# Memory rows and ride rows issued from ScalarE's queue, row pairs for the 64-row parts of T, and another order

## The chip, the cores and the metric

The kernel runs on one core of one Trainium2 chip. Its engines are TensorE (PE, with its weight loads as PEld), VectorE (DVE), ScalarE (ACT), GpSimd (POOL) and SyncE (SP), each with a queue of its own that is worked off in order. The metric is device time in microseconds (us) of one execution, as a median of several. A profiled execution gives the trace from which the durations below are read.

## The reference

Two layer pairs, each of them a recurrent attention A and a gated MLP B, on 2048 tokens of width 448:

```python
x = x + A(layernorm(x));  x = x + B(layernorm(x))
x = x + A(layernorm(x));  x = x + B(layernorm(x))

# A: 64 segments of 32 tokens, 16 heads of 256, memory of 8 rows
mem = mem0
for s in range(64):
    h = concat([mem, xs])                      # 40 rows
    q, k, v = h Wq, h Wk, h Wv                 # per head
    p = softmax(mask(q k^T / 16))
    o = sum over heads of (p v) Wo
    mem, out_s = o[:8], o[8:]
# B
h = relu(x W_gate) * (x W_up);  out = h W_down
```

The 8 memory rows of a segment are needed by the next one, so the segments of a layer form a chain. The two A layers use the same weights.

## The kernel before, in words

**Folded weights.** In the setup the kernel makes M = Wq Wk^T / 16 and N = Wv Wo for each head, so that a segment needs T = M h, the scores T^T h, U = p h and the output U N. M's 448 rows are cut into three parts of 128 and one of 64. The 64-row parts lie in the tensor M3, two blocks in one slot: one in partitions 0 to 63, one in 64 to 127 (PLACE, beside BLOCKS, L1042).

**Steps.** The program has 68 steps t (step, L1382). Step t works on segment t of layer 0 and on segment t - 4 of layer 1 side by side (LAG = 4), so most matmuls of T have 2 x 40 = 80 columns; in the first four and last four steps only one layer is at work, with 40. One step holds, by function:
- m_nat (L1201): six small DMAs that carry the memory rows mv, made by the step before. Four (L1211) put 8 rows by half the width each into hK, which the products U read; two (L1218) put 16 rows by half the width each into ride, from where L1221 (DVE) adds them to x of layer 1's rows in XB.
- t_block (L980), three times: T for blocks of units. Its inner function first() makes the 64-row parts of a block as matmuls that run beside each other in parts of the array, the rest the three 128-row parts. Each unit's PSUM bank is copied out by t_copies (L1024) into TTm and TTs, by ScalarE or DVE.
- s_mem (L1054), p_t_mem, u_mem, un_mem (L1158), m_t (L1178): the memory rows' attention and their output. un_mem is 112 matmuls; its halves are added by ScalarE (sumA) and DVE (mv, L1176). m_t transposes mv by matmuls, and DVE copies it into hT for the next step's T.
- s_seg (L1076), seg_pt, u_seg (L1231): the same for the segment's 32 rows. PTs is made by a DMA transpose. u_seg's four products per layer go to PSUM and are copied into big and UTm by ScalarE or DVE.
- In every second step un (L1274) makes U N for two segments, and then ln_b, b_layer, ln_a follow: layer norms, whose xBT and xAT come from DMA transposes (tdma, L975), and the MLP on a tile of 128 tokens.

**What sets the order.** No engine's order is written out. Each operation is recorded with the engines that may run it and a cost in ns (add); _Order.run (L391) is a list scheduler that takes the operations by due time (SLOT, keyed by function and step mod 4, period 86000 ns, with BIAS added) and by when its cost figures say that the engine, the PSUM bank and the inputs are free. For the steady steps (8 to 63) the TensorE order is pinned by SLOT. What comes out is one fixed instruction list for each engine, with semaphore waits (_Sched). Among the cost figures are 500 ns for a DMA issued from SP (qdma, L891), 1200 ns for a DMA transpose (tdma), and 120 ns for a DMA issued from ScalarE, which before the change only the six loads at the start use (small, L697). TensorE's cost figures have 95 ns for a change of tile shape ("mode": 0 full array, 1 for 64 rows by 128 columns, 2 for 32 columns, 3 for 64 by 64).

## Time and profile before

| | us |
|---|---|
| median of 3 runs | 1539.51 (1538.65 to 1540.07) |
| the profiled execution | 1535.5 |
| its span | 1533.6 |
| TensorE busy (matmul) | 1477.1 |
| VectorE busy | 803.6 |
| ScalarE busy | 777.2 |
| GpSimd busy | 112.8 |

The granted TensorE clock was 0.994 of full speed over the span. "Span" is the time from the first to the last instruction that the profile shows; the difference to the execution's own time lies around it. Issuing a DMA is not counted as busy time of an engine, but it occupies its queue: SP's queue held 461 copies and 146 transposes, ScalarE's six copies. Matmuls overlap, so the time of one kind is better read from the starts in the timeline than from its busy time. In the timelines a line has the start, the time until the last of the group ended, the engine (SPq and ACTq are queues that issue a DMA), the line of the code, the operation, output<-input, and the number of instructions.

### The profile page before, as it was taken

The numbers are of one execution on the slowest core, as the hardware profiler recorded it, in microseconds if no ns is written. First come the engines' busy times: TensorE is split into PE (matmuls) and PEld (weight loads), VectorE is DVE, ScalarE is ACT, GpSimd is POOL, SyncE is SP. The second block draws the span as 40 slices with busy tenths as digits, with TensorE's granted clock in tenths as the row PEclk, the third lists the DMA queues.
The fourth block names the chain that finished last, engine by engine and source line by source line (L and its number), as shares of the span: only waits on it lengthen the run. The fifth ranks groups of instructions, "written<-read, shape, count | busy, mean of one in ns | idle before, by whom it ended". The sixth has DMA issues, their size and how long they took to land.

```text
span 1533.6 us, 88464 instructions
## 1 busy us (share of the span) xinstructions
PE 1477.1 (96%) x41047; PEld 1157.1 (75%) x41051; DVE 803.6 (52%) x2198; ACT 777.2 (51%) x2491; POOL 112.8 (7%) x259
## 2 busy tenths in 40 slices
PE   6999889999999999999999999999999999999998
PEld 2577777878787887878687787878787788878675
DVE  6544545545554555645554554545455564555554
ACT  6644444555545554554555455554555455554433
POOL 4000000000000000000000000000000000000000
PEclk9999999999999999999999999999999999999999
DMA  9741001111110111111010110011010110011010
GB/s 219 185 126 29 17 16 22 22 16 19 22 22 16 24 17 21 22 17 19 16 24 17 24 21 16 19 22 22 17 24 17 22 22 17 18 20 21 17 21 14
DMA packets 137761, 48.24 MB, mean 31 GB/s; under 512 B 125736, under 2 KB 137264, under 8 KB 137392
## 3 DMA queue, kind: packets, MB, share of 16 engines
q1 hardware_dynamic: 137040, 42.33, 14.1%
q8 instruction: 323, 5.29, 1.4%
q14 instruction: 46, 0.38, 0.1%
q10 hardware_dynamic: 352, 0.24, 0.1%
HBM read 10.33 MB, written 1.84 MB: 8 GB/s over the span
## 4 chain that ended last, share of the span: by engine, by line
PE 83%; DVE 5%; DMA 4%; SPq 3%; ACT 3%; issue 1%
PE b L139 83%; SPq L690 3%; DMA PTs<-Ps 2%; DVE big L865 1%; DMA xBT<-xn 1%; ACT UTm L864 1%; ACT Em L1069 1%; DVE UTm L865 1%; DMA xAT<-xn 1%; SPq L1211 1%; DMA ride<-mv 0%; DVE mv L1176 0%; DVE Es L1111 0%; DMA Nw<-in_A_Wo_dram 0%; ACT sumA L864 0%
## 5 line engine op out<-in xcount | busy, mean ns | idle before, releaser
L139 PE MATMUL b<-hT,Mw 128*128 128x80 bf16 (+1 forms) x11424 | 438.6, 200 | 5.3 <-issue 4.1
L139 PEld LDWEIGHTS b<-hT,Mw 128*128 128x128 bf16 x11424 | 418.3, 100 | 19.2 <-issue 7.7
L139 PE MATMUL b<-Nw,big 128*32 128x448 bf16 (+1 forms) x3840 | 294.0, 353 | 1.9 <-DMA Nw<-in_A_Wo_dram 0.7
L864 ACT ACTIVATE TTm<-b 128x80 bf16<-128x80 f32 (+5 forms) x639 | 149.2, 234 | 273.8 <-PE b L139 266.1
L864 ACT ACTIVATE TTs<-b 128x320 bf16<-128x320 f32 (+5 forms) x640 | 269.0, 420 | 5.3 <-PE b L139 4.9
L139 PE MATMUL b<-xBT,big 128*128 128x128 bf16 (+3 forms) x4900 | 207.9, 215 | 4.1 <-DMA xBT<-xn 4.0
L139 PEld LDWEIGHTS b<-Nw,big 128*32 128x32 bf16 (+1 forms) x3840 | 131.3, 97 | 105.2 <-issue 10.3
L139 PE MATMUL b<-Nw,UTm 128*32 128x224 bf16 x7504 | 197.2, 263 | 6.4 <-ACT UTm L864 5.0
L139 PEld LDWEIGHTS b<-Nw,UTm 128*32 128x32 bf16 x7504 | 178.7, 98 | 29.3 <-ACT UTm L864 13.0
L139 PEld LDWEIGHTS b<-xBT,big 128*128 128x128 bf16 (+1 forms) x4900 | 182.6, 101 | 19.0 <-DMA xBT<-xn 4.7
L865 DVE CAST TTm<-b 64x64 bf16<-64x64 f32 (+4 forms) x245 | 54.6, 223 | 200.1 <-PE b L139 196.0
L139 PE MATMUL b<-hT,M 64*64 64x80 bf16 (+3 forms) x6808 | 145.9, 199 | 2.3 <-DVE hT L865 1.4
L864 ACT ACTIVATE big<-b 128x512 bf16<-128x512 f32 (+1 forms) x228 | 111.1, 544 | 60.8 <-PE b L139 60.4
L865 DVE CAST big<-b 128x512 bf16<-128x512 f32 (+1 forms) x160 | 97.3, 624 | 64.0 <-PE b L139 63.3
L139 PEld LDWEIGHTS b<-hT,M 64*64 64x64 bf16 (+2 forms) x6808 | 110.7, 107 | 26.6 <-issue 16.5
L864 ACT ACTIVATE UTm<-b 128x512 bf16<-128x512 f32 (+2 forms) x173 | 87.2, 541 | 64.8 <-PE b L139 64.0
L865 POOL COPY hK<-xn 32x448 bf16<-32x448 bf16 x136 | 75.3, 554 | 573.7 <-DVE xn L918 567.4
L865 DVE CAST TTs<-b 64x256 bf16<-64x256 f32 (+5 forms) x244 | 102.6, 420 | 5.4 <-PE b L139 5.4
L1343 DVE TENSOR_TENSOR hB<-gT,b 128x512 bf16<-128x512 bf16 (+2 forms) x128 | 78.0, 619 | 47.9 <-ACT gT L1342 26.8
L139 PE MATMUL b<-big,hB 128*128 128x448 bf16 (+1 forms) x574 | 100.0, 353 | 0.8 <-DVE hB L1343 0.8
L1342 ACT ACTIVATE gT<-b 128x512 bf16<-128x512 f32 (+2 forms) x128 | 66.4, 539 | 65.0 <-DVE hB L1343 34.1
L864 ACT ACTIVATE sumA<-b 64x224 f32<-64x224 f32 x67 | 23.7, 354 | 135.3 <-PE b L139 135.2
(101 smaller groups left out, 1328.6 us busy)
## 6 DMA issues: line engine op xcount, KB each, us to landing
hK<-mv SPq DMA_DIRECT2D x252, 3.5 KB
big<-in_A_Wo_dram SPq DMA_DIRECT2D x3, 896.0 KB, 5.9
ride<-mv SPq DMA_DIRECT2D x124, 7.0 KB, 1.8
out_dram<-ys SPq DMA_DIRECT2D x32, 56.0 KB, 2.0
big<-in_B_W_up_dram SPq DMA_DIRECT2D x7, 224.0 KB, 3.1
big<-in_B_W_gate_dram SPq DMA_DIRECT2D x7, 224.0 KB, 3.8
big<-in_B_W_down_dram SPq DMA_DIRECT2D x7, 224.0 KB, 3.4
XA<-in_A_x_dram SPq DMA_DIRECT2D x28, 56.0 KB, 2.2
```

The costliest lines, as they stand in the source:

```text
L139: ins = E.matmul(out, lhsT=lhsT, rhs=rhs, **kw)
L690: S.q.add("dma", ("sp",), {"sp": 6200.0 if w == "Wv" and q else 4100.0}, lambda E: E.dma_start_transpose(out=st[w, q], in_=src[w][:, q * 1 ...
L864: return E.activation(out(), src(), ACT.Copy, **({} if scale is None else {"scale": scale}))
L865: return E.tensor_copy(out(), src()) if scale is None else E.tensor_scalar(out(), src(), scale, None, op0=ALU.mult)
L1069: S.act(lambda E, i=i: E.activation(S.Em[:, i, :], src()[:, i, :], ACT.Exp, bias=st[:, 32 + i:33 + i], scale=1.0, accum_out=st[:, 34 + i:3 ...
L1211: S.qdma(f"mk{l}{n}", lambda E, a=a, b=b, n=n: E.dma_start(S.hK[a:a + 8, pp, s, DH * n:DH * n + DH], S.mv[b:b + 8, :]), [("hKm", pp, s, l, ...
L1342: S.act(lambda E, g=g, R=R, n=n: E.activation(S.gT[:, g, 0:n], R[0].b()[:, 0:n], ACT.Relu), n, R[0].res(), [("gT", g)])
L1343: S.dve(lambda E, g=g, R=R, n=n, fcs=fcs: E.tensor_tensor(S.hB[:, fcs[0]:fcs[-1] + 1, 0:w], S.gT[:, g, 0:n].rearrange("p (a b) -> p a b", ...
```

## The change

The six small DMAs of m_nat are recorded with adma and not qdma: ScalarE issues them, with a cost of 120 ns each in the scheduler. t_block's first() makes each 64-row part as one matmul of 64 rows by 128 columns of the array, two of which (partitions 0 to 63 and 64 to 127) stand in a pair, where two 64x64 matmuls each made it before. The tables BIAS and SLOT have new numbers; the period stays. The line numbers behind the tables grow by 2 to 5.

```diff
-    "t_blockm+": 4131, "t_blocks+": 6194, "s_mem+": -350, "p_t_mem+": 7632, ...
+    "t_blockm+": -901, "t_blocks+": -588, "s_mem+": -9244, "p_t_mem+": 9533, ...
...
+    def adma(self, name, fn, wr, rd=()):
+        self.q.add("dma", ("act",), {"act": 120.0}, fn, rd, wr, name=name, lat=2200.0)
...
                 for j in range(units[a][2]):
-                    for o, x in ((0, a), (0, b), (1, a), (1, b)) if l1 - l0 == 2 else ((-1, a), (-1, b)):
+                    for x in (a, b):
                         c, u0, m = units[x]
                         side, slot = S.PLACE[16 * c + u0 + j]
-                        h, g = slice(64 * side, 64 * side + 64), slice(64 * o, 64 * o + 64) if o >= 0 else slice(0, 128)
-                        out.append(MM(R[x].b()[g, j * n:j * n + n], S.M3[h, slot, g], mov(3, h), start=(j == 0), stop=False))
+                        h = slice(64 * side, 64 * side + 64)
+                        out.append(MM(R[x].b()[:, j * n:j * n + n], S.M3[h, slot, :], mov(3, h), start=(j == 0), stop=False))
...
-            S.mm(first, ..., mode=3 if l1 - l0 == 2 else 1)
+            S.mm(first, ..., mode=1)
...
-                S.qdma(f"mk{l}{n}", lambda E, a=a, b=b, n=n: E.dma_start(S.hK[a:a + 8, pp, s, DH * n:DH * n + DH], S.mv[b:b + 8, :]),
+                S.adma(f"mk{l}{n}", lambda E, a=a, b=b, n=n: E.dma_start(S.hK[a:a + 8, pp, s, DH * n:DH * n + DH], S.mv[b:b + 8, :]),
...
-                S.qdma(f"ride{n}", lambda E, a=a, b=b, n=n: E.dma_start(S.ride[a:a + 16, DH * n:DH * n + DH], S.mv[b:b + 16, :]), [("ride", w, n)], [("mem",)])
+                S.adma(f"ride{n}", lambda E, a=a, b=b, n=n: E.dma_start(S.ride[a:a + 16, DH * n:DH * n + DH], S.mv[b:b + 16, :]), [("ride", w, n)], [("mem",)])
```

## The prediction

> **What bounds the kernel now.** I read the page's busy shares first, then the chain of work that ended last, then the list of who waited for whom, and last the timelines of single steps.

> ```profile
> PE 1477.1 (96%) x41047; PEld 1157.1 (75%) x41051; DVE 803.6 (52%) x2198; ACT 777.2 (51%) x2491; POOL 112.8 (7%) x259
> ...
> PE b L139 83%; SPq L690 3%; DMA PTs<-Ps 2%; DVE big L865 1%; DMA xBT<-xn 1%; ACT UTm L864 1%; ACT Em L1069 1%; DVE UTm L865 1%; DMA xAT<-xn 1%; SPq L1211 1%; DMA ride<-mv 0%; DVE mv L1176 0%; DVE Es L1111 0%; DMA Nw<-in_A_Wo_dram 0%; ACT sumA L864 0%
> ```

> TensorE is busy 96% of the span and makes 83% of the chain, so the order keeps it fed. Adding up the gaps between matmul starts that exceed the usual gap of their kind gives some 39 us of stall in 1533.6 us, 1.2 us in a good period of four steps (86.6 us) and 2 to 3 us in a poor one (88.5 us). All that a better order can win lies in these 39 us; what makes TensorE wait longer is lost in full. Idle time of ScalarE (49%) is spread over the step, and whether it can take more work depends on when.

> **What the moved DMAs cost ScalarE.** The change moves 252 memory-row issues (hK<-mv) and 124 ride issues from SP to ScalarE, six per step. SP's own price for them, and what an issue from ScalarE takes (the only six in this trace, at the start), stand in the SP and ACT timelines; the source view of line 1211 has the spread:

> ```profile
> L1211 SPq DMA_DIRECT2D hK<-mv x252: 624/635/1480, 78.1 to 1503.2; - x126
> ```
> ```profile
> 1309.19 1.23 SPq L1218 DMA_DIRECT2D ride<-mv  x2
> 1310.46 3.25 SPq L1211 DMA_DIRECT2D hK<-mv  x4
> ```
> ```profile
> 0.75 1.28 ACT L629 ACT_TABLE_LOAD   x1 [0.75 <-PEq L1427]
> 0.78 0.56 ACTq L829 DMA_DIRECT2D XA<-in_A_x_dram  x1
> 1.37 0.77 ACTq L705 DMA_DIRECT2D ys<-in_A_mem_dram  x1
> 2.18 0.28 ACTq L706 DMA_DIRECT2D ys<-in_A_mem_dram  x1
> 2.50 1.77 ACTq L829 DMA_DIRECT2D XA<-in_A_x_dram  x3
> ```

> The reader is to see that issues stand one behind the other on ScalarE's queue as on SP's (0.78 + 0.56 ends at 1.34, the next begins at 1.37): 0.28 to 0.77 us each. What ran beside them was work already dispatched (the table load), nothing behind them. So the price per issue is bounded by 0.28 and 0.77 us; I take 0.66 us, the pitch of the same transfers on SP (0.635 us and 0.59 us busy, 0.67 and 0.62 us from one to the next), because rows, bytes and memories are the same. Six issues hold ScalarE's queue for 4 x 0.67 + 2 x 0.62 = 3.9 us. The planner that made the order counts 0.12 us each, 0.7 us for six: so the order leaves room for 0.7 us.

> [...]

> **What waits behind the six issues.** The order of the changed kernel is periodic: four kinds of step, the six issues in ScalarE's queue right after mv. A step of kind A (t mod 4 = 0) has the same TensorE order there as now, so the timelines of now (PE, ACT, DVE, SP) price it:

> ```profile
> 1284.47 0.84 PE L139 MATMUL b<-PTs,hK 40*64 40x512 bf16 x12
> ...
> 1286.83 0.53 PE L139 MATMUL b<-hT,M 64*64 64x80 bf16 x40
> 1287.29 1.36 PE L139 MATMUL b<-hT,Mw 128*128 128x80 bf16 x33
> ```
> ```profile
> 1284.59 0.35 ACT L864 ACTIVATE sumA<-b 64x224 f32<-64x224 f32 x1 [3.49 <-PE b L139]
> 1284.97 1.57 ACT L864 ACTIVATE UTm<-b 128x512 bf16<-128x512 f32 x3
> ```
> ```profile
> 1284.93 0.69 DVE L865 CAST big<-b 128x512 bf16<-128x512 f32 x1 [3.75 <-PE b L139]
> 1285.54 0.37 DVE L1176 TENSOR_TENSOR mv<-b,sumA 64x224 bf16<-64x224 f32 x1
> ```
> ```profile
> 1285.94 2.64 SPq L1211 DMA_DIRECT2D hK<-mv  x4
> ```

> Time from un_mem's end (1284.47): mv is done at +1.44, the first issue starts at +1.47, TensorE begins the next T block (hT,M) at +2.36, into banks that include the one of the third UTm eviction. Now that eviction ends at +2.07. In the changed order two UTm evictions stand ahead of the issues and the third behind them.

> - **A**: issues end at 1.47 + 3.9 = 5.4, the eviction (0.6 plus 0.1 of hand-over) at 6.1; TensorE could start at 2.36: stall 3.75 us.
> - **B** (t mod 4 = 1): issues right after sumA and mv, 0.9 to 4.85; then an eviction of big, done at 5.5. TensorE has ahead of the U product that reads it 8 x 0.38 (8 matmuls 128x448 each, 56 such in 2.66 us) + 0.45 (u_seg) = 3.5 us: stall 2.0 us.
> - **C** (mod 2): issues to 4.85, relu 0.4, four pairs TTm and TTs of 0.54 each, done at 7.5. TensorE ahead of the block that needs those banks: 30 gate/up matmuls x 0.056, m_t 0.2, ten row pairs 0.37, 84 matmuls x 0.0366, switches 0.3 = 5.6 us: stall 1.9 us.
> - **D** (mod 3): four issues, three evictions, two issues; the evictions end at 5.2, TensorE asks at 5.2: stall 0 to 0.1 us.

> That is 7.7 us per four steps, and 14 periods (t = 8 to 62) have it: 108 us. The first steps and the last carry the same issues in another order; I count nothing for them. After each burst ScalarE catches up within the T blocks (in A its queue is done with the first five banks at 9 us, when TensorE asks), so a stall isn't paid twice. By the bounds: at 0.28 us each A stalls 1.5 us and the others nothing, 21 us in all; at 0.77 us the four stall 4.45, 2.7, 2.6 and 0.4 us, 142 us in all.

> **What the moved DMAs free.** SP loses 376 issues, 246 us of issue time (252 x 0.66 and 124 x 0.64), so its transposes (xBT, xAT, PTs), x loads and y stores no longer stand behind them. What is that worth? In poor periods the chain runs from mv over four hK issues and a ride issue to the ride's landing (2.1 us) and the xBT transpose (4.2 us), where TensorE waits 1.1 us. On ScalarE the ride still stands behind the four memory rows, so this chain grows no shorter; but a TensorE held up by 3.75 us no longer waits at its end. I count 10 us of today's 39 us of stall as covered by the new ones or gone with SP's queue, between 0 and 20. The landing of the memory rows is no issue: the next u_mem reads them over 10 us later.

> **Row pairs.** In each step 100 matmuls 64x64 (25 sets of four) become 50 of 64 rows by 128 columns; 3000 matmuls and weight loads go. But a set of four takes 37.8 to 38.9 ns now (40 matmuls in 0.36 us), because four run beside each other. The trace has the new shape at 40 columns, in the first steps:

> ```profile
> 93.84 0.42 PE L139 MATMUL b<-hT,M 64*128 64x40 bf16 x20
> 94.19 1.40 PE L139 MATMUL b<-hT,Mw 128*128 128x40 bf16 x48
> ```

> Twenty in 0.35 us with the switch behind them: 25.4 ns a pair, what one full 128x128 matmul takes at 40 columns. So at 80 columns a pair should take the 36.6 ns of a full one: 25 x 1.7 ns x 60 steps = 2.5 us less. A change of tile shape costs 95 ns beyond the pitch between 64x64 and full, 83 to 87 ns for 64x128: 4 x 10 ns x 60 = 2.4 us less; the new order has 818 such changes instead of 803, 1.4 us more. Together -3 us; were the pairs to run singly it would be +55 us, which the row excludes.

> **The order.** Apart from the burst it differs little: as many evictions (ScalarE 22 more, DVE 22 fewer), 112 quarter matmuls for 28 full ones in un. Nothing for it, +-10 us.

> **Sum**, against the profiled execution (1535.5 us, of which 1533.6 span): 1535.5 + 108 - 10 - 3 = 1630.5; the median lies 4.0 above that execution: **1635 us**. In this case 1605 to 1668.

> **Rivals.**
> - *The issue is cheap on ScalarE (faster).* If an issue holds ScalarE's queue for under 0.13 us, as the planner counts, A stalls less than 6 x 0.13 - 0.18 = 0.6 us per period, below what SP's queue and the pairs give back; then 1539.5 - 3 - 10 = 1526 us. Place: the time from mv's end to the next ScalarE activation. For it: SP's queue is on the chain (1%) and goes. Against it: the six ACT rows, the shortest of them 0.28 us. Chance 0.12, nearly all below 1536.
> - *Short issues.* 0.28 to 0.5 us, like the shortest ACT row: 1539.5 + 21 - 13 = 1548 up to 1605. Chance 0.15, a fifth of it within 0.2%.
> - *Both queues hold each other up.* On SP a ride behind a transpose took up to 1.5 us instead of 0.59; if ScalarE's first issue pays that 0.9 us beside SP's transposes in A, B and C, 2.7 us per period come on top, 38 us: 1673 us. Chance 0.15.
> - The forecast's own case: 0.58.

> Faster by over 0.2% (what a measurement of this kernel can tell from no change) 0.12, within it 0.03, slower 0.85. The range reaches from the end of the short issues to the third rival, 1540 to 1675 us: it leaves out the 0.12 below and half of the 0.15 above.

> **What the profile after would show.** Right: ACT queue rows hK<-mv and ride<-mv of 0.6 us, each time six in a row; TensorE waiting for ScalarE's UTm, big and TTs evictions, 3 to 4 us at the hT,M block after m_t in every fourth step; a period of 92 to 95 us; ScalarE's busy time unchanged, as issues don't count; 64x128 pairs at 37 ns. Wrong: activations that begin within 1.4 us of mv in kind A, or a period below 87 us.

## The result, and the profile after

| | before | after |
|---|---|---|
| median, us | 1539.79 (4 runs, 1538.65 to 1550.1) | 1695.05 (4 runs, 1690.79 to 1698.62) |
| ratio | | 1.099, 95% interval 1.0934 to 1.1047 |
| span of the profiled execution, us | 1533.6 | 1690.4 |
| granted TensorE clock over the span | 0.994 | 0.966 |

The change makes the kernel 10% slower. The forecast was 1635 us with a range to 1675: the direction is right, the size 60 us too small, and the range misses it. The busy shares and the chain of the kernel after:

```profile
PE 1520.3 (90%) x38135; PEld 1189.2 (70%) x38135; DVE 795.0 (47%) x2176; ACT 779.6 (46%) x2513; POOL 112.6 (7%) x259
...
PE 67%; ACTq 10%; DVE 9%; ACT 6%; DMA 3%; SPq 3%; issue 2%
PE b L139 67%; ACTq L1216 7%; ACTq L1223 3%; SPq L692 3%; DMA PTs<-Ps 2%; DVE big L867 2%; ACT TTs L866 1%; ACT big L866 1%; DVE mv L1181 1%; DVE UTm L867 1%; ACT sumA L866 1%; ACT Em L1074 1%; DVE hB L1348 1%; ACT UTm L866 1%; ACT TTm L866 1%
```

ScalarE's issues, which were not on the chain, now make 10% of it, and ScalarE's busy time is 2.4 us off what it was (issues are not counted). One thing in the first line fits no stall: 2912 matmuls fewer, and yet PE is busy 43 us longer. The waits of TensorE, by what ended them (total us, times, longest):

```profile
PE b L139 <- ACT UTm L866: 55.3, 17, 4.0
PE b L139 <- ACT big L866: 37.7, 27, 2.6
PE b L139 <- ACT TTs L866: 28.6, 16, 3.4
```

These are the three evictions that the prediction named. Before, the largest entry of this kind was:

```profile
PE b L139 <- ACT UTm L864: 5.0, 16, 0.9
```

The source views of the two lines that issue (min/median/max in ns):

```profile
L1216 ACTq DMA_DIRECT2D hK<-mv x252: 631/652/2037, 78.2 to 1655.7; - x126
```
```profile
L1223 ACTq DMA_DIRECT2D ride<-mv x124: 514/607/1575, 175.8 to 1654.4; - x124
```

One step of kind A, ScalarE's and then TensorE's timeline:

```profile
1019.82 0.35 ACT L866 ACTIVATE sumA<-b 64x224 f32<-64x224 f32 x1 [3.49 <-PE b L139]
1020.20 1.08 ACT L866 ACTIVATE UTm<-b 128x512 bf16<-128x512 f32 x2
1021.17 2.78 ACTq L1216 DMA_DIRECT2D hK<-mv  x4
1023.98 1.18 ACTq L1223 DMA_DIRECT2D ride<-mv  x2
1025.21 0.60 ACT L866 ACTIVATE UTm<-b 128x512 bf16<-128x512 f32 x1 [3.92 <-DVE XB L1293]
```
```profile
1021.92 0.30 PE L139 MATMUL b<-PTs,hK 40*64 40x256 bf16 x4
1025.95 0.85 PE L139 MATMUL b<-hT,M 64*128 64x80 bf16 x20 [3.72 <-ACT UTm L866]
1026.73 2.38 PE L139 MATMUL b<-hT,Mw 128*128 128x80 bf16 x33
```

Two UTm evictions, then six issues for 4.0 us, and only then the third UTm eviction, for whose bank TensorE waits 3.72 us: the stall of kind A, as worked out. But the next two groups show what was not: the 20 matmuls of 64 rows (ten pairs) and the 33 full ones begin 0.78 us apart, where before the same block of 64-row parts took 0.46, and the 33 last 2.38 us instead of 1.36 (one starts 67 ns after the other instead of 36). TensorE runs at about half its speed there. The windows view of this stretch (width, busy us of each engine, granted clock, DMA) has it:

```profile
1021.27:1024.68 3.41, 0.96 (x29) 0.33 (x28) 3.13 (x7) 0.01 (x1) 0.19 (x1) 1.00 0.09 21
1024.68:1028.10 3.42, 2.15 (x41) 2.06 (x42) 0.56 (x2) 1.79 (x6) 0.00 (x0) 0.50 0.02 4
1028.10:1031.51 3.41, 3.41 (x56) 3.41 (x53) 0.61 (x2) 2.00 (x8) 0.00 (x0) 0.50 0.02 5
1031.51:1034.92 3.41, 3.41 (x109) 3.28 (x107) 1.05 (x4) 2.56 (x10) 0.00 (x0) 1.00 0.19 38
...
1055.40:1058.81 3.41, 3.41 (x60) 1.64 (x52) 0.23 (x1) 0.00 (x0) 0.19 (x1) 0.50 0.01 2
```

The clock is 1.00 until 1024.68, in the middle of the stall, then 0.50 for 6.8 us, in which the work behind the stall runs, and 0.50 again behind the 2.2 us stall of the next step (kind B). With TensorE busy all of a 3.41 us stretch, the rows count 109 matmuls at full clock and 56 at half (all of the 56, but only 79 of the 109, use all 128 rows; the other 30 run in pairs). The PEclk row of the profile's page, the clock in 40 slices, is all nines, since a slice is 42 us long: only the mean clock (0.966) and short windows show this.

**Where the 157 us of span are.** From the trace, over the 14 periods from t = 7 to t = 63 (1221.9 us before, 1366.6 after, 144.7 more):

| part | us |
|---|---|
| gaps without a running matmul: 17.6 before, 122.8 after | +105.2 |
| matmuls running at half clock: 3.4 us before, 86.7 us after (8.9 us of half clock lie in the gaps); estimate: half of the difference is lost | +41.7 |
| the rest (row pairs, order) | -2.2 |

The remaining 12 us lie in the first and last steps (head 209.8 before, 217.4 after; tail 101.9 and 106.4). A second trace of the kernel before has a head of 216.8 us, so those of the head are scatter, as far as two traces tell.

### The profile page after: what moved, and what is told of

It is laid out like the page before. It is cut to its first block, busy times and chain, and to the rows that moved or that the text cites. A ratio compares the mean times of both kernels' runs of the same rounds, so it can differ in the third digit from the quotient of the medians.

```text
span 1690.4 us, 82676 instructions
## 1 busy us (share of the span) xinstructions
PE 1520.3 (90%) x38135; PEld 1189.2 (70%) x38135; DVE 795.0 (47%) x2176; ACT 779.6 (46%) x2513; POOL 112.6 (7%) x259
## 4 chain that ended last, share of the span: by engine, by line
PE 67%; ACTq 10%; DVE 9%; ACT 6%; DMA 3%; SPq 3%; issue 2%
PE b L139 67%; ACTq L1216 7%; ACTq L1223 3%; SPq L692 3%; DMA PTs<-Ps 2%; DVE big L867 2%; ACT TTs L866 1%; ACT big L866 1%; DVE mv L1181 1%; DVE UTm L867 1%; ACT sumA L866 1%; ACT Em L1074 1%; DVE hB L1348 1%; ACT UTm L866 1%; ACT TTm L866 1%
## 5 line engine op out<-in xcount | busy, mean ns | idle before, releaser
L139 PE MATMUL b<-hT,Mw 128*128 128x80 bf16 (+1 forms) x11424 | 468.4, 205 | 1.4 <-DVE M L867 1.2
L139 PEld LDWEIGHTS b<-hT,Mw 128*128 128x128 bf16 x11424 | 450.2, 103 | 19.0 <-DVE M L867 1.6
L139 PE MATMUL b<-Nw,big 128*32 128x448 bf16 (+1 forms) x3924 | 308.1, 361 | 32.5 <-ACT big L866 31.5
L866 ACT ACTIVATE TTs<-b 128x320 bf16<-128x320 f32 (+5 forms) x665 | 283.8, 432 | 1.1 <-PE b L139 1.0
L866 ACT ACTIVATE TTm<-b 128x80 bf16<-128x80 f32 (+5 forms) x665 | 159.6, 240 | 228.8 <-PE b L139 222.7
L139 PE MATMUL b<-hT,M 64*128 64x80 bf16 (+3 forms) x3808 | 153.8, 202 | 88.1 <-ACT UTm L866 52.3
L139 PEld LDWEIGHTS b<-Nw,big 128*32 128x32 bf16 (+1 forms) x3924 | 129.8, 98 | 139.3 <-ACT big L866 37.8
L139 PE MATMUL b<-xBT,big 128*128 128x128 bf16 (+3 forms) x4900 | 213.0, 216 | 2.0 <-ACT xBT L866 0.7
L139 PE MATMUL b<-Nw,UTm 128*32 128x224 bf16 x7504 | 195.8, 262 | 4.2 <-ACT UTm L866 1.6
L139 PEld LDWEIGHTS b<-xBT,big 128*128 128x128 bf16 (+1 forms) x4900 | 185.4, 102 | 18.7 <-issue 4.1
L139 PEld LDWEIGHTS b<-Nw,UTm 128*32 128x32 bf16 x7504 | 177.7, 98 | 25.3 <-issue 11.3
L139 PEld LDWEIGHTS b<-hT,M 64*128 64x128 bf16 (+1 forms) x3808 | 112.6, 100 | 116.8 <-issue 57.9
L1347 ACT ACTIVATE gT<-b 128x512 bf16<-128x512 f32 (+1 forms) x128 | 66.8, 543 | 121.7 <-issue 68.8
L139 PE MATMUL b<-big,hB 128*128 128x448 bf16 (+1 forms) x574 | 101.2, 353 | 1.3 <-DVE hB L1348 1.1
L867 DVE CAST TTs<-b 64x256 bf16<-64x256 f32 (+4 forms) x219 | 88.9, 406 | 3.0 <-PE b L139 2.9
L139 PE MATMUL b<-PTs,hK 40*64 40x512 bf16 (+1 forms) x1024 | 76.5, 361 | 9.2 <-DMA PTs<-Ps 5.5
```

The costliest lines, as they stand in the source:

```text
L139: ins = E.matmul(out, lhsT=lhsT, rhs=rhs, **kw)
L866: return E.activation(out(), src(), ACT.Copy, **({} if scale is None else {"scale": scale}))
L867: return E.tensor_copy(out(), src()) if scale is None else E.tensor_scalar(out(), src(), scale, None, op0=ALU.mult)
L1347: S.act(lambda E, g=g, R=R, n=n: E.activation(S.gT[:, g, 0:n], R[0].b()[:, 0:n], ACT.Relu), n, R[0].res(), [("gT", g)])
```

## The experiments

Theory (Q, where an expectation uses a letter): ScalarE's queue is held 0.65 us by each issue, what stands behind six of them comes late, TensorE waits, and after the wait its clock is halved for one or more stretches of 3.41 us. Rivals: the new order or the row pairs cost the time; or SP's queue and ScalarE's hold each other up. Ratios are to runs of the kernel before on the same chip, since its median differs from chip to chip (1539 to 1544 us). The first four runs were e1, e2, e3 and e5; the others were chosen after their results.

### The issues back on SP

```diff
-                S.adma(f"mk{l}{n}", ...
+                S.qdma(f"mk{l}{n}", ...
-                S.adma(f"ride{n}", ...
+                S.qdma(f"ride{n}", ...
```

> The changed kernel with its new tables and its row pairs, but the memory rows and ride rows issued from SP again. Theory Q (ScalarE's queue is held by the issues, and TensorE's clock is halved after the stalls): 1522 to 1538 us, granted clock 0.99, no wait of TensorE on an eviction over 1 us. Rival O (the new order or the row pairs are slow by themselves): over 1600 us. Rival M (they carry a third or more of it): 1570 to 1600 us.

Measured: 1529.38 us, ratio 0.9919 (0.9893 to 0.9945), clock 0.993. New tables and row pairs without the issues are 0.8% faster than before: all of the loss belongs to the issues. The trace allows a closer comparison, since TensorE's 31220 matmuls of the steady stretch are the same here and in the changed kernel, in the same order: 1212.4 us here, 154.2 us more there. Of these, 111.6 us are gaps (11.2 here, 122.8 there) and 42.6 us matmuls that follow each other more slowly, 38.6 of them while the clock is halved. So the price of the halved clock is read from the trace and not only estimated.

### The issues alone

The kernel before, with adma (120 ns) for the six DMAs and nothing else.

> The kernel before, with the memory rows and ride rows issued from ScalarE and nothing else changed. Theory Q: 1640 to 1710 us, in step A six issues between the second and the third UTm eviction and a stall of 3.5 to 4 us, granted clock 0.95 to 0.975. Rival O: 1535 to 1560 us.

Measured: 1683.37 us, ratio 1.0924 (1.0872 to 1.0976), clock 0.966, 112.6 us at half clock in 27 stretches. The waits are the same three:

```profile
PE b L139 <- ACT UTm L864: 57.6, 32, 4.1
PE b L139 <- ACT big L864: 36.5, 20, 3.5
PE b L139 <- ACT TTs L864: 23.4, 17, 2.2
```

The moved issues cost 9% with the old tables; with the new tables and the row pairs it is 11% (1.0991 against 0.9919).

### The row pairs alone

```diff
-                    for o, x in ((0, a), (0, b), (1, a), (1, b)) if l1 - l0 == 2 else ((-1, a), (-1, b)):
+                    for x in (a, b):
...
-                        out.append(MM(R[x].b()[g, j * n:j * n + n], S.M3[h, slot, g], mov(3, h), start=(j == 0), stop=False))
+                        out.append(MM(R[x].b()[:, j * n:j * n + n], S.M3[h, slot, :], mov(3, h), start=(j == 0), stop=False))
```

> The kernel before with the 64-row parts of T as row pairs and nothing else changed. Theory Q: 1530 to 1542 us, a pair in 36.5 to 37 ns where a set of four took 38 to 39. Rival P (the pairs run slower than the sets of four or lower the clock): over 1560 us.

Measured: 1527.68 us, ratio 0.9913 (0.9878 to 0.9948): better than expected. Since it is level with the first experiment, the new tables by themselves bring nothing that can be measured. The surprise was run again in more rounds:

> The kernel before with the row pairs alone, once more, in more rounds. The pitches in the trace give 2.5 to 5 us less than before (20 ns for each of 120 groups, and cheaper changes of shape): ratio 0.997 to 0.998. The first comparison gave 0.9913 [0.9878, 0.9948]. If the pairs also spare stalls, the ratio is 0.990 to 0.994 again; if the first comparison was the scatter of poor periods, 0.996 to 0.999.

Measured: 1532.05 us, ratio 0.9923 (0.9893 to 0.9953). So the gain is 12 us, not 3. Then three traces from one chip, of the kernel before, the pairs, and the kernel before:

> The kernel before, unchanged, for a trace from the same chip as the next run. If the 12 us that the row pairs gain come from the pitches alone, this trace and that of the pairs differ by 3 to 5 us in span, as the traces at hand do (1533.6 and 1530.4); if they come from periods with stalls, this one has more periods of 87.2 us and above (8 of 14 in the trace at hand, 2 of 14 with the pairs) and a span 8 to 16 us longer.

> The kernel before with the row pairs alone, beside the run of the kernel before. By the pitches alone the span is 3 to 5 us shorter than that run's; if fewer poor periods are the cause, 8 to 16 us, with at most 4 of 14 periods of 87.2 us and above.

> The kernel before once more, to tell what two traces of one kernel differ by: 3 us or less in span and the same number of poor periods within two, if the periods are a property of the order; more, if they are chance.

Measured: spans 1533.0, 1526.1 and 1537.5 us. Two traces of one kernel differ by 4.5 us in span, so single traces can't settle 3 against 12; over all traces, though, the steady stretch is 1220.2 to 1221.9 us in the three of before and 1213.1 to 1219.0 in the three with pairs, the median period 87.04 to 87.22 against 86.49 to 86.67, and periods of 87.2 us and above are 8, 7 and 4 of 14 against 3, 2 and 1. A group of 15 pairs (30 matmuls) takes 20 ns less than its 15 sets of four, and so does one of ten; 120 such groups make 2.4 us. The gaps fall from 16.3 to 17.6 us to 10.2 to 14.4, 2 to 7 us more. A line in the waits moves with them; first the kernel before, then the pairs, on one chip:

```profile
PE b L139 <- issue: 5.3, 13, 1.0
```
```profile
PE b L139 <- issue: 2.0, 5, 0.9
```

These are waits for nothing that the profile shows; they became fewer along with the 3000 matmuls and weight loads. Whether fewer instructions are the cause was not tried. The predicted 3 us are the pitches, and fewer small stalls add 2 to 7 us in the traces. What is left of the 12 stands in no trace: the three spans of the pairs are 4.7 us shorter in the mean than those of before, and the profiled runs of the first two comparisons were among the slower ones (1532.18 and 1535.22 us, with medians of 1527.68 and 1532.05).

### Filling the stalls

The changed kernel, with matmuls whose results nobody reads put on TensorE ahead of the groups that wait (128x128 by 512 columns: 16 in kind A, 9 in B, 6 in C, 5 in D of the steady steps). The computation is whole; TensorE has more to do.

```diff
+                n = self.FILL.get(o.slot, 0) if 2 * LAG <= o.t < NSEG else 0
+                if n:
...
+                    self.sc.pe([MM(K.banks[b][:, 0:512], K.ident[:, :], K.M[:, 0, 0:4, :], start=True, stop=True) for _ in range(n)], [], [("ps", b, 0), ("ps", b, 1)])
```

> The changed kernel with idle-time work on TensorE: in each steady step some matmuls of 512 columns, whose results nobody reads, ahead of the group that waits (16 in A, 9 in B, 6 in C, 5 in D, 7.8 us in four steps, about as long as the stalls). They neither remove a wait nor an issue. If the stalls cost what they last plus a halved clock after them (theory Q): half-clock time falls from 116 us to under 40 us, granted clock 0.985 to 0.995, 1640 to 1665 us. If the clock has no part in it, or follows something other than TensorE's idle time: 1685 to 1710 us.

Measured: 1666.78 us, ratio 1.0808 (1.0772 to 1.0845), clock 0.992, half clock 27.3 us, where the changed kernel has 116.2. The busy shares:

```profile
PE 1596.6 (96%) x38639; PEld 1200.2 (72%) x38639; DVE 795.1 (48%) x2176; ACT 776.5 (47%) x2513; POOL 113.0 (7%) x259
```

Kind A, TensorE's timeline:

```profile
1013.38 3.63 PE L139 MATMUL b<-Mw,ident 128*128 128x512 bf16 x16
1017.17 0.54 PE L139 MATMUL b<-hT,M 64*128 64x80 bf16 x20 [0.17 <-ACT UTm L874]
1017.64 1.36 PE L139 MATMUL b<-hT,Mw 128*128 128x80 bf16 x33
```

504 matmuls that do nothing useful make the kernel 28 us faster. Nothing on ScalarE changed, its queue is held as long, and TensorE goes on no earlier than in the changed kernel (the T block begins 6.26 us after un_mem's end, there 6.25); what is gone is the halved clock, and the 33 matmuls take 1.36 us again. The time lies 2 us above the expected range, since a fill that outlasts its stall delays what follows. The steady stretch is 26 us shorter and not 42, because the fills and the gaps that are left (21.8 us, where the changed kernel has 9.2 beside its stalls) are together longer than the stalls were. This is a probe and not a remedy: the stalls, now filled, stay.

### Two of six issues on ScalarE

The changed kernel with qdma for mk (the memory rows) and adma for ride alone.

> The changed kernel with the memory rows back on SP; the two ride copies a step still go from ScalarE. Theory (ScalarE's queue is held 0.66 us by each issue, and TensorE's clock halves only after stalls that leave it idle for most of a 3.41 us stretch): two issues hold 1.24 us. Kind A: third UTm eviction done 1.47 + 1.24 + 0.7 = 3.4 us after un_mem's end, TensorE asks at 2.36: stall 1.05 us; the other kinds 0. 14 x 1.05 = 15 us above the 1529 of the run with all issues on SP: 1544 us (1532 to 1552), and half-clock time stays near the 16 to 23 us of the kernels that issue from SP. Rival (loss goes with the number of issues, whatever their place, two of six): 1529 + 166 / 3 = 1584 us and some 50 us at half clock.

Measured: 1544.69 us, ratio 1.0002 (0.9984 to 1.002), clock 0.993, 20.9 us at half clock. Kind A again, ScalarE's and TensorE's timeline:

```profile
938.27 1.09 ACT L866 ACTIVATE UTm<-b 128x512 bf16<-128x512 f32 x2
939.24 1.16 ACTq L1223 DMA_DIRECT2D ride<-mv  x2
940.45 0.60 ACT L866 ACTIVATE UTm<-b 128x512 bf16<-128x512 f32 x1 [1.10 <-PE b L139]
```
```profile
940.00 0.30 PE L139 MATMUL b<-PTs,hK 40*64 40x256 bf16 x4
941.19 0.54 PE L139 MATMUL b<-hT,M 64*128 64x80 bf16 x20 [0.90 <-ACT UTm L866]
941.66 1.36 PE L139 MATMUL b<-hT,Mw 128*128 128x80 bf16 x33
```

The stall is 0.92 us in the mean of 14 periods (1.05 expected), 12.9 us in all; against the run with all issues on SP the ratios differ by 0.83%, 12.8 us. The 33 matmuls behind it last 1.36 us: full clock. A third of the issues cost 8% of what six cost (12.8 of 165 us), so it is not their number that counts, but what stands behind them and how long TensorE is left idle.

### The planner told the price

```diff
-        self.q.add("dma", ("act",), {"act": 120.0}, fn, rd, wr, name=name, lat=2200.0)
+        self.q.add("dma", ("act",), {"act": 660.0}, fn, rd, wr, name=name, lat=2200.0)
```

> The changed kernel, with the planner told 660 ns instead of 120 ns for an issue from ScalarE; all six issues stay there, but the order puts evictions between them. Kind B: big's eviction stands behind two issues and not six, done at 0.9 + 1.3 + 0.65 = 2.9 us, before TensorE asks (3.5): stall 0. Kind C keeps its six issues ahead of the four TTm/TTs pairs: 1.6 us as measured after. A and D: 0 to 1 us each, no UTm eviction stands behind the issues in A any more. 1.6 to 3.6 us a period, 22 to 50 us, and 0 to 25 us by half clock after those: 1551 to 1604 us, 1575 taken. Rival (the order makes no difference, the 250 us of issue time must be paid somewhere since ScalarE is on the path): 1660 to 1700 us. Rival (a planner that knows the price hides all of it): 1525 to 1535 us.

Measured: 1551.81 us, ratio 1.0052 (1.003 to 1.0074), clock 0.996, 13.7 us at half clock. ScalarE still issues all six DMAs a step, 254 us of its queue in all, and 145 us of the loss are gone (ratio 1.0052 against 1.0991). In kind A:

```profile
943.64 1.09 ACT L866 ACTIVATE UTm<-b 128x512 bf16<-128x512 f32 x2
944.62 2.67 ACTq L1216 DMA_DIRECT2D hK<-mv  x4
947.32 0.54 ACTq L1223 DMA_DIRECT2D ride<-mv  x1
947.90 0.24 ACT L866 ACTIVATE TTm<-b 128x80 bf16<-128x80 f32 x1 [3.17 <-DVE big L867]
948.01 0.54 ACTq L1223 DMA_DIRECT2D ride<-mv  x1
```
```profile
946.00 0.53 PE L139 MATMUL b<-hT,M 64*128 64x80 bf16 x20 [0.33 <-DVE UTm L867]
```

The third UTm eviction went to VectorE, whose busy time rose from 795.0 to 873.6 us, and TensorE waits 0.33 us for it. The time is at the lower end of what was expected; compared with the issues on SP (ratio 0.9919), 1.3% or 20 us remain, 16.6 of them as gaps in the steady stretch (27.8 against 11.2 us).

### The issues on GpSimd

```diff
+    def gdma(self, name, fn, wr, rd=()):
+        self.q.add("dma", ("pool",), {"pool": 1000.0}, fn, rd, wr, name=name, lat=2200.0)
```

Used for mk and ride, in the kernel with row pairs alone.

> The kernel before with the row pairs, and the six small DMAs issued from GpSimd, whose queue is 7% busy; SP is relieved as in the change, ScalarE is not burdened. The prediction put SP's relief at 10 us (0 to 20). Theory: the ride still lands behind the memory rows, so the chain to xBT is hardly shorter: 0 to 10 us below the 1527.7 of the pairs alone, 1518 to 1528 us. Rival (an issue from GpSimd takes longer or lands later than one from SP): xBT comes later and TensorE waits in every second step, 1535 to 1560 us.

Measured: 1535.77 us, ratio 0.9943 (0.9925 to 0.996), against 0.9923 (0.9893 to 0.9953) with the pairs and SP on the same chip. That is above the expected 1518 to 1528 us: SP's relief gains nothing. The steady stretch is 1213.3 us (1213.1 in the best trace of the pairs), the tail 108.7 against 101.9 to 102.5. The page has what the issues take there (busy us, mean ns), and the median landing in us:

```profile
L1214 POOL DMA_DIRECT2D hK<-mv x252 | 130.6, 523 | 376.2 <-DVE mv L1179 344.6
...
hK<-mv POOLq DMA_DIRECT2D x252, 3.5 KB, 1.9
...
ride<-mv POOLq DMA_DIRECT2D x124, 7.0 KB, 2.7
```

Here nobody of importance stands behind them; the ride lands after 2.7 us, against 2.2 to 2.6 from SP in the three traces of the pairs.

## Why the prediction was wrong, point by point

- **Price of an issue: right.** 0.66 us taken; 0.65 and 0.61 us measured, one behind the other. The cheap and the short issue are both excluded.
- **Stalls of A, B and C: right.** 3.75, 2.0 and 1.9 us predicted; 3.74, 2.06 and 1.91 measured as means of 14 periods.
- **Stall of D: too small.** 0 to 0.1 us predicted, 0.40 measured as a mean: 3 of the 14 periods have one of 1.1 to 1.5 us. In two of them single issues took longer (in one, the four memory rows lasted 3.82 us instead of 2.78 and TensorE waited 1.26 us); in the third all six issues stood ahead of the three evictions. 20 of the 376 issues on ScalarE last over 0.8 us; on SP, before, it was 25.
- **The four together: 108 us predicted, 113.6 measured.**
- **Today's stalls, -10 us: the size holds, the reason does not.** Of 17.6 us of steady gaps before, 9.2 remain beside the stalls. But SP's relief is worth nothing (on GpSimd the issues gained none), and the row pairs alone take 3 to 7 of them.
- **Row pairs, -3 us: too small.** -12 us alone (ratios 0.9913 and 0.9923); the pitches are about as predicted (36.4 and 36.7 ns a pair in groups of 15 and ten, 37.4 and 38.2 a set of four), the change to the full shape is no cheaper at 80 columns (131 ns from start to start behind pairs and behind sets), the fewer small stalls were not counted, and part of the 12 is not explained. The 818 changes of tile shape, put down to the new order, come with the pairs (818 also in the pairs alone). In the changed kernel little of it can be seen (ratio 1.0991, and 1.0924 with the issues alone).
- **Order, 0: right.** Ratio 0.9919 with the new tables, 0.9913 with the old.
- **The step that failed: a stall was counted for only as long as it lasts.** The sum goes from "stall 3.75 us" straight to "7.7 us per four steps"; the work behind a stall was taken at full clock. Some 42 us of the steady stretch are the halved clock, 45 us over the whole span (90 us more of matmuls at half clock, half of them lost). That is three quarters of the 60 us by which the forecast was short; the rest are gaps, of which it had 98 us more (108 - 10) and the trace has 114, 8 of them in the first and last steps, for which it counted nothing. The halved clock belongs beside the stalls (7.7 us per period predicted, 8.1 measured), as 3.0 us more.
- **The third rival**, whose 1673 us come closest, names a cause that is not there: long issues are no more common on ScalarE than on SP, and the stalls of A, B and C hold nothing of the 0.9 us that it adds to each.

The prediction could have known. In the trace of before, the windows view has the same thing in the head, behind a stretch in which TensorE was busy 0.67 of 3.41 us:

```profile
206.35:209.76 3.41, 0.67 (x21) 0.35 (x17) 2.89 (x9) 2.75 (x10) 0.00 (x0) 1.00 0.02 5
209.76:213.17 3.41, 3.40 (x76) 2.86 (x80) 0.00 (x0) 0.00 (x0) 0.00 (x0) 0.50 0.19 38
213.17:216.58 3.41, 3.20 (x96) 1.89 (x92) 1.86 (x5) 2.22 (x6) 0.09 (x1) 1.00 0.03 7
```

Four more stretches at half clock lie in that trace; the mean clock of 0.994 made them look like nothing. That the change would add long stalls to every period was known, and the price of one stood in this view.

## What to carry to other kernels

In the trace after, an issue on ScalarE took 0.65 us (a ride 0.61) in the median, the next issue began 0.03 us behind its end, and during 348 of the 376 no activation began, so what counts is which instructions stand behind it: two issues behind which one eviction waited cost 0.8%, six cost 9 to 11%, and six with the evictions moved out of their way 1.3%. Tell the scheduler the measured price of an issue (0.12 against 0.66 us was worth 145 us here), and price a TensorE stall of 2 us or more above its own length (here half clock followed 24 of 36 stalls of 1.9 to 2.6 us, and 33 of 34 longer ones), at up to 1.7 us for each 3.41 us stretch of half clock behind it, an estimate: half of the stretch. The best version found is the kernel before with the row pairs and the issues left on SP: ratios 0.9913 and 0.9923.

## What the runs showed of the hardware

| TensorE busy in a stretch | stretches | next one at half clock |
|---|---|---|
| under 40% | 58 | 58 |
| 40 to 60% | 97 | 50 |
| 60 to 80% | 203 | 26 |
| over 80% | 5493 | 1 |

  The one exception in the last row is itself a stretch at half clock (e6_ride_act, from 95.79 us). A stall need not fill a stretch. From 60 us on, a stall of 3.5 us or more was followed by the halved clock each time (27 of 27; wherever it falls, one stretch is more than half idle), one of 2.6 to 3.5 us in 6 of 7 cases, one of 1.9 to 2.6 us in 24 of 36, one of 1.3 to 1.9 us in 7 of 47, and of e6_ride_act's 14 stalls of 0.92 us in the mean none. Busy here is what the records show. That the place of a stall in the grid decides is a reading of the table and was not tested by itself; why the middle rows are mixed was not shown.
- What makes a long issue (over 0.8 us) on ScalarE or SP stays open. After the change 18 of the 20 begin 1.3 to 6 us after a DMA transpose was issued, but so do 240 of all 376 issues, and before it was 17 of 25 against 266 of 376. All 376 issues from GpSimd took 0.48 to 0.65 us.
